# Decay scans per 128 tokens with laid-out zero columns, mirrored upper features, a first mixing in two groups, and fillers to the idlest bank

## The chip, the core and the metric

One core of a Trainium2 chip runs the whole program. The metric is device time of one execution in microseconds (us). The engines are TensorE (PE: matmuls and transposes), VectorE (DVE), ScalarE (ACT) and GpSimd (POOL); SyncE (SP) issues most of the DMAs. Each engine takes its instructions in the order of its own queue and waits on semaphores where an operand isn't ready.

## What is computed

Batch 4, 8 heads, 768 tokens, head size 48, 384 features. A linear attention with a decay per token and channel gives `x`; then comes the real part of a 2D FFT over tokens and features as mixing, a norm, and a feed-forward network (FFN) of 384 to 1536 to 384:

```python
def _attn_ref(q, k, v, alpha) -> np.ndarray:
...
    for t in range(S):
        state = alpha[:, :, t, :, None] * state + np.einsum('bhd,bhe->bhde', k[:, :, t], v[:, :, t])
        y[:, :, t] = np.einsum('bhd,bhde->bhe', q[:, :, t], state)
...
def _moe_ref(x, w_ch1, w_ch2) -> np.ndarray:
    X = np.fft.fft(x, axis=1)
    X = np.fft.fft(X, axis=2)
    mixed = np.real(X).astype(np.float32)
    u = x + mixed
    mu = np.mean(u, axis=-1, keepdims=True)
    var = np.mean((u - mu) ** 2, axis=-1, keepdims=True)
    un = (u - mu) / np.sqrt(var + 1e-06)
    ch = np.maximum(un @ w_ch1, 0.0) @ w_ch2
    return (u + ch).astype(np.float32)
```

## The kernel before, in words

**Order of the work.** Operations are not issued where they are written. A class `Plan` (from line 193) records every one with its operands and a priority, and `emit` (378) is a list scheduler: it fixes, from a table of assumed durations and delays, the order of each engine's queue and which slot each tile gets, and then issues everything from one place (L508 in the profile; relu L229). So a change of one operation can move many others. `FX` (523) names the engines that may take a kind of operation.

**Fillers.** While the planned time is below `WARM` (120 us), a planned gap of TensorE is filled with matmuls of a zero tile (L1237; one for every 0.11 us, `DUMMY`), written to a part of a PSUM bank that nothing reads. The bank is the first in a list that holds no open accumulation (466). A filler's bank may still be waiting to be read by another engine; then the filler waits, and the queue behind it.

**Attention** runs by pairs of heads (four pairs a batch; 0 to 3 are batch 0), in stages `s1` to `s8` of `attn_stages` (700). The decays of a pair are a tile `al`, 112 rows (two heads) by 768 tokens. `products` in `s1` makes running products of decays `w` by a scan on VectorE (`w<-al,d`) and the inverse weights by a second scan backwards (`al<-al,back`). The scans restart every 64 tokens: ScalarE copies every 64th decay into the scan's addend `d1` (`d<-al`), GpSimd sets these places of `al` to zero (in pair 0 VectorE does both), and since the chunks that the matmuls use have 128 tokens, VectorE multiplies the first half of each by the reciprocal of its end product (`rec`, `w<-w,rec`) and makes the decay of a chunk, `mt`, as a product of two values. `s2`, `s3` multiply keys and queries into the scans (`al<-kq,al`, `w<-kq,w`); `s4` transposes the keys (`f<-cst,al`, ScalarE copies `kt`); `s5` computes scores in a chunk and masks them (VectorE, `x<-f,cst`, in batch 0); `s6` the states, carried from chunk to chunk (`tc<-f,mt` and four steps `tc<-tc,mt`, ScalarE copies `tt`); `s7` the outputs, copied by ScalarE into the tiles `y`.

**Mixing.** The DFT over tokens is folded by sums of `y` (`combine`, 859: `z<-y,y`, `sd<-z`, `z<-sd,z`) ahead of small matmuls (`token_stage`), then the DFT over features, again by matmuls. In batch 0 `first_mix` (891) does this by groups of 128 features as soon as the pairs are there: group 0 after pair 1, group 1 after pair 2, group 2 after pair 3; each adds its part of the second stage to three open PSUM banks (`a<-f,x`, 193 and 191 columns). `adds` (976) adds the result to `y` in four VectorE steps per block of 128 rows: the lower features, and the upper ones in reversed order. The upper half of the tokens goes through a DRAM scratch (`scr`) and comes back with its rows reversed by indirect DMAs of GpSimd.

**FFN.** The weights come packed; `wsplit` (677) unpacks each block: ScalarE makes `b8` and a sign, VectorE a shift and an `or`, ScalarE an absolute value, VectorE or GpSimd a product, ScalarE the high part, VectorE or GpSimd the low part. The DMA of a further block waits until a slot is free. The norm (`norm_stages`, 1003) ends in transposes and casts to `x`; the first FFN matmul is the first `f<-x,wt`. From there the FFN of a batch and the attention and mixing of the next share TensorE.

Of the kernel before, what the change touches and what calls it, by code (L numbers as in the profile page):

```python
# [21 lines left out]
DM = H * D  # L22
# [4 lines left out]
C = 64  # L27
NW = 2 * DFF // P
NC = S // C
HM = DM // 2  # L30
CW = 112
# [22 lines left out]
SPLIT = 388  # L54
# [7 lines left out]
P4 = 512 - DM  # L62
# [40 lines left out]

def first_tables():
    p = np.arange(P, dtype=np.int64)[:, None]
    t = []
    for g in range(DM // P):
        x = 2.0 * np.pi * (((P * g + p) * np.arange(HM + 1)[None, :]) % DM) / DM
        t += [np.cos(x), np.sin(x[:, 1:HM])]
    return np.ascontiguousarray(np.concatenate(t, axis=1).astype(np.float32))  # L110
# [20 lines left out]

class View:
# [8 lines left out]
    def __getattr__(self, name):  # L141
        if name not in ("rearrange", "bitcast", "broadcast_to"):
            raise AttributeError(name)
        return lambda *a, **k: View(self.tile, self.steps + ((name, a, k),))

    def real(self, base=None):
        ap = self.tile.real if base is None else base
        for name, a, k in self.steps:
            ap = getattr(ap, name)(*a, **k)
        return ap  # L150
# [32 lines left out]
KEEP = {'c8': 0, 'a': 1, 'f1': 1, 'f2': 1, 'b8': 0, 'y': 3, 'mv': 99, 'st': 99, 'sd': 99, 'r3': 99, 'kq': 2}  # L183
# [9 lines left out]
class Plan:  # L193


    def __init__(self, engines):
        self.engines, self.ops, self.tags, self.direct, self.key, self.chain, self.fill = engines, [], {}, None, 0.0, None, False
        self.idle, self.open, self.both, self.half = None, set(), None, None
# [34 lines left out]
    def add(self, engines, name, args, kwargs):  # L233
# [8 lines left out]
        op.free, op.fill = 1, self.fill  # L242
# [135 lines left out]
    def emit(self):  # L378
# [35 lines left out]
        while placed < len(ops):  # L414
            placed += 1
            best = None
            for e, cand in wait.items():
# [17 lines left out]
                for key, n, late in sorted((ops[n].key, n, late) for t, late, n in times):  # L435
# [3 lines left out]
                    limit = min(limit, late + DELAY[e])  # L439
# [25 lines left out]
            if op.engine == "PE" and self.idle and t < self.idle[2]:  # L465
                bank = next((x for x in self.idle[3] if x not in self.open), None)
# [16 lines left out]
            for slot in op.slots:  # L483
                slot.touched.append(end)
                if slot.tag and len(slot.touched) == slot.uses:
# [37 lines left out]
FX = {'comb': 'V', 'mul': 'V', 'first': 'V', 'wm': 'VG', 'wd': 'VG', 'fold': 'V', 'ev': 'A', 'relu': 'A', 'un': 'V', 'hi': 'A', 'xh': 'A', 'er': 'AV', 'kl': 'V'}  # L523
# [4 lines left out]
def gla_mix_ffn(ctx: ExitStack, tc: tile.TileContext, alpha, kq, v, w1, w2, consts, tables, rowtab, out):  # L528
# [12 lines left out]
        "w3": ([P, 776], F32, NW3), "kt": ([P, NT - 1, CW], F32, 1),  # L541
        "z": ([P, 6, DM], F32, 1), "f": ([P, 6, DM], F32, 1), "sd": ([P, 8 * D], F32, 1), "h": ([P, S], F32R, 3), "x": ([P, 776], F32R, 6),
        "y": ([P, 3, DM], F32, NY), "b8": ([P, S], I8, 1), "c8": ([P, S], I8, 1), "st": ([P, 3, 6], F32, 2), "mv": ([P, 3, 2], F32, 2),
        "r3": ([P, 3], F32, 6),
        "al": ([P, 776], F32, NAL), "kq": ([P, 2, S], F32, NQK), "vn": ([P, VW], F32, NVN), "a": ([P, 512], F32, 3), "f1": ([P, 512], F32, 2), "f2": ([P, 512], F32, 3),
# [42 lines left out]
    mts = [fixed([P, NT], f"mt{i}") for i in range(3)]  # L588
    d1 = fixed([P, S], "d1")
    back = fixed([P, S], "back")  # L590
    rec = fixed([P, NC], "rec")
    bad = fixed([P, B * NP2], "bad")
    cm63 = fixed([P, 1], "cm63")
    ceps = fixed([P, 1], "ceps")
    zero = fixed([P, 32], "zero")
# [4 lines left out]
    scratch = [plan.fixed(dp.tile([DM, DM], F32, name=f"scr{b}")) for b in range(B)]  # L600

    def load_first():
        t, kt, vn = plan.tile("al"), plan.tile("kq"), plan.tile("vn")
        loaded.update({("al", 0): t, ("kq", 0): kt, ("vn", 0): vn})
        for lo, o in ((0, 0), (DM, SPLIT)):
            SY.dma_start(t[:, o : o + DM], alpha[0, :, lo : lo + DM])
# [5 lines left out]
    def check_first():  # L612
        t = plan.tile("h").bitcast(F32)
        SY.dma_start(t[:, 0:S], alpha[0])
        check(0, t)

    def check(p, t):
        top = t[0:CW, 0:S].bitcast(U8)[:, 3::4]
        A.activation(plan.tile("c8")[0:CW].bitcast(U8), top, AF.Square, bias=cm63[0:CW], accum_out=bad[0:CW, p : p + 1])

    def load_alpha(p):
        if p < B * NP2:
            t = plan.tile("al")
            loaded["al", p] = t
            SY.dma_start(t[:, 0:S], alpha[p])
# [18 lines left out]
    def setup():  # L644
        V.memset(zero, 0.0)
        A.activation(bs, zero[:, 0:1], AF.Sqrt)
        V.memset(d1, 0.0)
        for x in tts:
            G.memset(x, 0.0)
        V.memset(back, 0.0)  # L650
        V.memset(back[:, C - 1 :: 2 * C], 1.0)
        V.memset(cm63, -63.0)
        V.memset(ceps, 1e-6)
        for x in mts:
            V.memset(x, 0.0)
# [44 lines left out]
    def attn_stages(b, hp, i, mixed):  # L700
        tt, mt = tts[0], mts[hp % 3]
        pair = b * NP2 + hp
        e = {}
        halves = "p (c h t) -> p c h t"

        def products(lo, hi):
            as_, Af, o = loaded["al", pair], e["A"], off(lo)
            d, d2, chunks = d1[0:CW, lo:hi], back[0:CW, lo:hi], slice(lo // C, hi // C)
            if pair:
                A.copy(d[:, 0::C], as_[0:CW, o : o + hi - lo : C])  # L710
            else:
                same(d[:, 0::C], as_[0:CW, o : o + hi - lo : C])
            (G if pair else V).memset(as_[0:CW, o : o + hi - lo + 1 : C], 0.0)
            part = Af[0:CW, lo:hi]
            V.tensor_tensor_scan(out=part, data0=as_[0:CW, o : o + hi - lo], data1=d, initial=0.0, op0=ALU.mult, op1=ALU.add)
            r = rec[0:CW, chunks][:, 0::2]
            V.reciprocal(d2[:, 2 * C - 1 :: 2 * C], part[:, 2 * C - 1 :: 2 * C])
            V.reciprocal(r, part[:, C - 1 :: 2 * C])
            j0, j1 = max(lo // P - 1, 0), hi // P - 1
            V.tensor_mul(mt[0:CW, j0:j1], Af[0:CW, j0 * P + P - 1 : j1 * P : P], Af[0:CW, j0 * P + P + C - 1 : j1 * P + C : P])  # L720
            V.tensor_tensor_scan(
                out=as_[0:CW, o + hi - lo : o : -1], data0=as_[0:CW, o + hi - lo : o : -1], data1=d2[:, ::-1],
                initial=0.0, op0=ALU.mult, op1=ALU.add,
            )
            first = part.rearrange(halves, h=2, t=C)[:, :, 0]
            FL["first"].tensor_mul(first, first, r[:, :, None].broadcast_to([CW, (hi - lo) // P, C]))

        def off(t):
            return t + SPLIT - DM if pair == 0 and t >= DM else t

        def R(rows, lo, hi):
            return loaded["al", pair][rows, off(lo) + 1 : off(lo) + 1 + hi - lo]

        def times(which, x, lo, hi):
            FL["mul"].tensor_mul(x, loaded["kq", pair][0:CW, which, lo:hi], x)

        parts = ((0, DM), (DM, S)) if pair == 0 else ((0, S),)

        def s1():
            e["A"] = w3()[:, 0:S]  # L740
            if pair:
                check(pair, loaded["al", pair])
                products(0, S)
            else:
                products(0, DM)
                times(0, R(slice(0, CW), 0, DM), 0, DM)
                products(DM, S)

        def s2():
            lo = 0 if pair else DM  # L750
            times(0, R(slice(0, CW), lo, S), lo, S)

        def s3():
            for lo, hi in parts:
                times(1, e["A"][0:CW, lo:hi], lo, hi)

        def s4():
            kt = plan.tile("kt")
            e["kt"] = kt
            for a0, a1 in ((0, 3), (3, NT - 1)):  # L760
                pk = psa()
                for a in range(a0, a1):
                    T.transpose(pk[:, (a - a0) * P : (a - a0) * P + CW], R(slice(0, CW), a * P, (a + 1) * P), ident[0:CW, 0:CW])
# [3 lines left out]
        def s5():  # L767
            e["X"] = []
            for h2 in range(2):
# [4 lines left out]
                for c in range(3):  # L774
                    cs = slice((3 * h2 + c) * P, (3 * h2 + c + 1) * P)
# [612 lines left out]
```

## Time and profile before

| | us |
|---|---|
| median of 3 runs (lowest, highest) | 526.02 (525.55, 526.42) |
| the profiled execution | 527.16 |
| its span | 525.1 |
| TensorE busy (share of the span) | 503.6 (96%) |
| VectorE busy | 336.4 (64%) |
| ScalarE busy | 194.5 (37%) |
| GpSimd busy | 60.3 (11%) |

The profile is one execution. "Busy" counts instructions at work; in brackets behind a row of the timeline stands how long the engine was idle just before it and what ended that. TensorE's share is a mean over two very different parts: the head, up to the first FFN matmul, where its busy time holds the fillers, and all that follows. "PEclk" is the clock granted to TensorE, 1.00 or 0.50 in stretches of about 3.4 us.

### The profile page before, as it was taken

Reading aid. Unit: us, or ns where it says so; the run is one execution under the profiler, and the core shown is the slowest. Engines: PE = TensorE matmul, PEld = TensorE weight load, DVE = VectorE, ACT = ScalarE, POOL = GpSimd, SP = SyncE. Lnnn points to the kernel's source line nnn. Section 1 sums busy time; section 2 is a strip of 40 time slices with the busy share of each in tenths; the row PEclk is TensorE's granted clock in tenths of the full one; section 3 lists DMA queues with packets and bytes.
Section 4 is the critical chain, followed back from the end, with each engine's and each line's share of the span. In section 5 each row is a group of like instructions: output and inputs, shape, how many; then the busy total and the mean of one; then the engine's idle time right before and its main releaser. Section 6 shows DMA issues by size and latency. Waiting matters only on the chain.

```text
span 525.1 us, 10047 instructions
## 1 busy us (share of the span) xinstructions
PE 503.6 (96%) x4128; PEld 482.0 (92%) x4128; DVE 336.4 (64%) x757; ACT 194.5 (37%) x409; POOL 60.3 (11%) x84
## 2 busy tenths in 40 slices
PE   8799996999999999899999999999999999999995
PEld 7688886999999999799999999999999999999994
DVE  8878789799795798956529985755355824122112
ACT  2264566436556323634333152333322332111110
POOL 0001142042011200301212000212120000000000
PEclk9699899899999999999999999999999999999999
DMA  8992055022342510213226100120012001001001
GB/s 313 410 404 71 1 155 178 1 91 76 123 183 85 165 56 0 96 43 115 86 92 212 61 2 0 46 85 25 1 66 71 1 1 45 1 0 46 1 0 51
DMA packets 17267, 45.40 MB, mean 86 GB/s; under 512 B 1920, under 2 KB 7168, under 8 KB 17216
## 3 DMA queue, kind: packets, MB, share of 16 engines
q1 hardware_dynamic: 16160, 42.21, 22.4%
q0 software_dynamic: 768, 2.36, 1.6%
q8 instruction: 34, 0.56, 0.4%
q10 hardware_dynamic: 288, 0.13, 0.1%
q14 instruction: 17, 0.14, 0.1%
HBM read 37.62 MB, written 7.08 MB: 85 GB/s over the span
## 4 chain that ended last, share of the span: by engine, by line
PE 84%; DVE 6%; DMA 4%; ACT 3%; issue 1%; POOL 1%; SPq 0%; ACTq 0%; DVEq 0%
PE f L508 62%; PE a L508 20%; DMA wt<-in_w_dram 3%; PE f L1237 2%; DMA al<-in_alpha_dram 2%; DVE w L508 1%; DVE wt L508 1%; DVE x L508 1%; DVE y L508 1%; ACT c L508 1%; DVE tc L508 1%; ACT wt L508 0%; ACT b L508 0%; ACT f L508 0%; POOL wt L508 0%
## 5 line engine op out<-in xcount | busy, mean ns | idle before, releaser
L508 PE MATMUL f<-x,wt 128*128 128x384 f32 x864 | 180.4, 345 | 1.7 <-ACT x L508 1.7
L508 PE MATMUL f<-wt,h 128*128 128x384 f32 x864 | 176.4, 342 | 0.7 <-ACT h L229 0.7
L508 PEld LDWEIGHTS f<-x,wt 128*128 128x128 f32 x864 | 150.5, 189 | 3.7 <-ACT x L508 2.0
L508 PEld LDWEIGHTS f<-wt,h 128*128 128x128 f32 x864 | 150.3, 188 | 1.8 <-ACT h L229 1.0
L508 DVE SCALAR_TENSOR_TENSOR h<-f,h 128x384 fp32r<-128x384 f32 x96 | 53.2, 554 | 118.8 <-ACT h L229 117.9
L229 ACT ACTIVATE h<-f 128x384 fp32r<-128x384 f32 x96 | 47.2, 491 | 167.0 <-PE f L508 166.3
L508 POOL TENSOR_SCALAR_AFFINE_SELECT w<-w 128x384 f32<-128x384 f32 x48 | 34.4, 738 | 161.8 <-ACT w L508 161.8
L508 PE MATMUL a<-vn,w 128*128 128x80 f32 x288 | 43.4, 271 | 0.1
L508 PEld LDWEIGHTS a<-vn,w 128*128 128x128 f32 x288 | 39.8, 191 | 1.1 <-POOL al L508 0.2
L508 ACT COPY w<-a 128x384 f32<-128x384 f32 (+4 forms) x60 | 26.6, 481 | 33.0 <-PE a L508 31.4
L1237 PEld LDWEIGHTS f<-zero 128*32 128x32 f32 x650 | 25.9, 124 | 12.8 <-ACT x L508 3.7
L1237 PE MATMUL f<-zero 128*32 128x32 f32 x650 | 28.7, 208 | 9.1 <-ACT x L508 3.3
L508 DVE TENSOR_TENSOR_SCAN w<-al,d 112x768 f32<-112x768 f32 (+1 forms) x17 | 29.1, 1711 | 7.0 <-PE a L508 3.9
L508 DVE TENSOR_TENSOR y<-y,a 128x191 f32<-128x191 f32 (+4 forms) x106 | 30.4, 340 | 1.8 <-PE a L508 1.7
L508 DVE TENSOR_TENSOR_SCAN al<-al,back 112x768 f32<-112x768 f32 (+1 forms) x17 | 28.2, 1659 | 0.0
L508 DVE TENSOR_TENSOR z<-y,y 128x576 f32<-128x576 f32 (+1 forms) x18 | 11.8, 686 | 20.8 <-ACT y L508 20.8
L508 PE MATMUL a<-w,al 64*128 64x128 f32 (+1 forms) x288 | 22.5, 289 | 0.0
L508 PEld LDWEIGHTS a<-w,al 64*128 64x128 f32 (+1 forms) x288 | 18.0, 187 | 4.5 <-ACT w L508 2.2
L508 POOL DMA_INDIRECT y<-scr,rows x12 | 16.0, 1334 | 50.5 <-DMA scr<-y 38.3
L508 PE MATMUL a<-tt,w 112*128 112x96 f32 x120 | 21.4, 276 | 0.0
L508 DVE SCALAR_TENSOR_TENSOR tc<-tc,mt 112x48 f32<-112x48 f32 x64 | 18.7, 292 | 0.7
L508 ACT COPY y<-a 128x288 f32<-128x288 f32 x24 | 9.5, 397 | 25.6 <-PE a L508 25.6
(112 smaller groups left out, 564.4 us busy)
## 6 DMA issues: line engine op xcount, KB each, us to landing
kq<-in_kq_dram SPq DMA_DIRECT2D x13, 768.0 KB, 5.2
wt<-in_w_dram SPq DMA_DIRECT2D x8, 768.0 KB, 8.2
al<-in_alpha_dram SPq DMA_DIRECT2D x15, 384.0 KB, 5.3
out_dram<-y SPq DMA_DIRECT2D x24, 192.0 KB, 1.9
vn<-in_v_dram SPq DMA_DIRECT2D x14, 304.0 KB, 3.2
wt<-in_w_dram SPq DMA_DIRECT2D x8, 384.0 KB, 6.7
scr<-y SPq DMA_DIRECT2D x4, 576.0 KB, 3.7
wt<-in_kq_dram SPq DMA_DIRECT2D x2, 768.0 KB, 10.9
```

The source lines that it names most:

```text
L229: return lambda out, x: e.activation(out, x, AF.Relu)
L508: op.ins = op.fns[op.engine](*[real(a) for a in op.args], **{k: real(x) for k, x in op.kwargs.items()})
L1237: lambda tag, i: nc.tensor.matmul(warm[tag][i][0:32, 480:512], zero.real(), zero.real(), start=True, stop=True), 1.0, WARM,
```

## The change

1. **Scans per 128 tokens.** The host lays the decays out with a zero column ahead of each 128 tokens (tile width 776 in place of 768, a row of 129 per chunk), and the addend `d1` is a constant with a one at these columns. A scan so restarts by itself every 128 tokens, over 773 columns. `d`, the memsets of `al`, `rec`, `mt` as a product and `w<-w,rec` are gone; ScalarE copies the last column of each chunk into a new tile `over`, which serves as `mt`, and a check of `over` for overflow is added at the end.
2. **Mirrored upper features.** The host reverses the upper 192 features (weights, values, and the result), and the `y` tiles get a padding column (385 wide, set to zero by GpSimd). A reversed step over the upper half becomes a forward one, and both halves go in one instruction (`twice`). Where the second stage's banks hold sum and difference already (batch 0), `adds` is one step per block of rows; elsewhere three. Stores write two runs of 192 features per row.
3. **First mixing in two groups**, after pairs 1 and 3, each of 96 lower and the 96 mirrored upper features. `combine` works on 192 columns; new folds (`h<-z`, sum and difference of a feature and its mirror) come ahead of the token matmuls, which need 24 instructions in place of 36, with 97 rows. The second stage has 12 matmuls of 386 columns in place of 18 of 191 or 193, and two short ones per group as before.
4. **Fillers** move 48 columns in place of 32 and go to the bank whose last planned read is earliest. Some keys and delays of the planner change (`TIGHT`, `KN0`, `KEEP`).

The core of the diff:

```diff
-C = 64
...
+CP = P + 1
+AW = NT * CP + 2
+YW = DM + 1
...
+FW = 48
...
+        def products(c0, c1):
+            al, Af = loaded["al", pair][0:CW], e["A"][0:CW]
+            lo, hi = c0 * CP + 1, c1 * CP + 1
+            V.tensor_tensor_scan(out=Af[:, lo : hi - 1], data0=al[:, lo : hi - 1], data1=d1[0:CW, lo : hi - 1], initial=1.0, op0=ALU.mult, op1=ALU.add)
+            last = Af[:, lo + P - 1 : hi - 1 : CP]
+            V.reciprocal(back[0:CW, lo + P : hi : CP], last)
+            FL["mt"].copy(mt[0:CW, c0:c1], last)
+            V.tensor_tensor_scan(
+                out=al[:, hi - 1 : lo : -1], data0=al[:, hi - 1 : lo : -1], data1=back[0:CW, hi - 1 : lo : -1], initial=0.0, op0=ALU.mult, op1=ALU.add,
+            )
...
-                A.copy(d[:, 0::C], as_[0:CW, o : o + hi - lo : C])
...
-            (G if pair else V).memset(as_[0:CW, o : o + hi - lo + 1 : C], 0.0)
...
-            V.reciprocal(r, part[:, C - 1 :: 2 * C])
...
-            V.tensor_mul(mt[0:CW, j0:j1], Af[0:CW, j0 * P + P - 1 : j1 * P : P], Af[0:CW, j0 * P + P + C - 1 : j1 * P + C : P])
...
-            FL["first"].tensor_mul(first, first, r[:, :, None].broadcast_to([CW, (hi - lo) // P, C]))
...
         def s8():
             if b == 0:
                 key = plan.key
-                if hp:
+                if hp % 2:
                     plan.key += KFM
-                    first_mix(hp - 1, *mixed())
+                    first_mix(hp // 2, *mixed())
...
     def first_mix(g, ytiles, zt):
...
-        combine(ytiles, zt, g * P, P, FL["comb"])
-        zs = [zt[:, i, cols] for i in range(6)]
+        combine(ytiles, zt, g, FL["comb"])
+        c0, n = 2 * D * g, 2 * D
+        folds = []
+        for f in (V.tensor_add, V.tensor_sub):
+            x = plan.tile("h").bitcast(F32)[:, 0 : 6 * HR].rearrange("p (a n) -> p a n", a=6)
+            f(x[:, :, 1:n], zt[:, :, c0 + 1 : c0 + n], zt[:, :, c0 + HM : c0 + HM + n - 1])
+            same(x[:, :, 0 : n + 1 : n], zt[:, :, c0 : c0 + HM + n : HM + n - 1])
+            folds.append(x)
...
-            T.matmul(pm[:, HM + 1 : DM], rt[1][:, ks], t[:, HM + 1 : DM], start=g == 0, stop=False)
+            T.matmul(pm[:, 0:PQ], rt[1][0:HR, ks], sn, start=g == 0, stop=False)
...
-            V.tensor_add(lo, lo, m1)
-            first(lo[:, 1:HM], lo[:, 1:HM], m2)
-            V.tensor_add(hi, hi, m1[:, 1:HM])
-            second(hi, hi, m2)
+            both = feats(u)
+            if pms:
+                x = pm[:, HM + 1 : HM + 2].twice(-HM, HM) if flip else pm[:, 0:1].twice(HM + 2, HM)
+                V.tensor_add(both, both, x)
+                return
...
-                bank = next((x for x in self.idle[3] if x not in self.open), None)
+                bank = min((x for x in self.idle[3] if x not in self.open), key=lambda x: self.read.get(x, 0.0), default=None)
```

Two places of the queues follow. A row is one instruction or several alike (x24): output, inputs, shape, and the engines or DMA queues that it waits for; the numbers tell tiles apart.

TensorE's queue early in the head, around the output matmuls of pair 0 (`f_..<-vn,x`; `x` are masked scores), before: rows with `zero` are fillers, and bank `f_1_50` also holds the states that VectorE's first `tc` step reads.

```order
L508 MATMUL f_1_50_115<-vn_42_107,kt_6_71 48x48
L1237 MATMUL f_2_51_116<-zero 32x32 [waits DVE_49]
L1237 MATMUL f_2_51_116<-zero 32x32 x4
L508 MATMUL f_2_68_352<-vn_42_107,x_13_78 128x80 [waits PE_49]
L1237 MATMUL f_1_50_115<-zero 32x32 [waits DVE_49]
L1237 MATMUL f_1_50_115<-zero 32x32 x24
L508 MATMUL f_2_68_352<-vn_42_107,x_13_78 128x80 x3
L508 MATMUL f_0_70_392<-vn_42_107,x_14_79 128x80
```

The same place now:

```order
L1281 MATMUL f_1_48_113<-zero 32x48 x3
L530 MATMUL f_0_68_321<-vn_42_107,x_13_78 128x80 [waits DVE_49]
L530 MATMUL f_0_68_321<-vn_42_107,x_13_78 128x80 x2
L1281 MATMUL f_1_50_115<-zero 32x48 x14
L530 MATMUL f_1_69_347<-vn_42_107,x_14_79 128x80 [waits DVE_49,PE_49]
L1281 MATMUL f_1_48_113<-zero 32x48 x2
```

The fillers that waited for VectorE, one on the mask's bank and 25 on the bank of the states, are gone from ahead of the output matmuls; those in their place carry no wait, while the output matmuls themselves wait for the masks.

VectorE's queue from the scan of pair 2 (`w_2`) to the scan of pair 3 (`w_3`), before; `al_38` and `al_39` are the decays of these pairs, and a wait for Pool is one for GpSimd's memset (further `tc` steps, alike, are left out):

```order
L508 SCALAR_TENSOR_TENSOR w_2_3_68<-al_38_103,d_135 112x768 [waits DMAHW4_49,Pool_49]
L508 SCALAR_TENSOR_TENSOR tc<-tc,mt_132 112x48 [waits DVE_49]
L508 RECIPROCAL back<-w_2_3_68 112x6 [waits DVE_49]
L508 RECIPROCAL rec<-w_2_3_68 112x6
L508 TENSOR_TENSOR mt_134<-w_2_3_68 112x5
L508 SCALAR_TENSOR_TENSOR al_38_103<-al_38_103,back 112x768 [waits DVE_49]
L508 TENSOR_TENSOR w_2_3_68<-w_2_3_68,rec 112x6x64 [waits DVE_49]
L508 SCALAR_TENSOR_TENSOR tc<-tc,mt_132 112x48
L508 TENSOR_TENSOR w_1_2_67<-kq_41_106,w_1_2_67 112x768
L508 SCALAR_TENSOR_TENSOR w_3_4_69<-al_39_104,d_135 112x768 [waits DMAHW0_49,Pool_49]
```

And now, left out in the same way:

```order
L530 SCALAR_TENSOR_TENSOR w_2_3_68<-al_38_103,d_133 112x773 [waits DMAHW4_49]
L530 SCALAR_TENSOR_TENSOR tc<-tc,over 112x48 [waits DVE_49]
L530 RECIPROCAL back<-w_2_3_68 112x6 [waits DVE_49]
L530 SCALAR_TENSOR_TENSOR al_38_103<-al_38_103,back 112x773 [waits DVE_49,Activation_49]
L530 TENSOR_TENSOR w_1_2_67<-kq_41_106,w_1_2_67 112x6x128
L530 SCALAR_TENSOR_TENSOR w_3_4_69<-al_39_104,d_133 112x773 [waits DMAHW0_49]
```

The rows `rec`, `mt` and `w<-w,rec` are gone from between the two scans, and the scan of pair 3 waits for its DMA alone, no longer for GpSimd.

More of the change, by code (lines that the diff above doesn't have):

```diff
@@ L197, in __init__ @@
         self.engines, self.ops, self.tags, self.direct, self.key, self.chain, self.fill = engines, [], {}, None, 0.0, None, False
-        self.idle, self.open, self.both, self.half = None, set(), None, None
+        self.idle, self.open, self.both, self.half, self.tight = None, set(), None, None, False
+        self.read = {}
     def tag(self, name, count, make):
@@ L484, in emit @@
                 slot.touched.append(end)
+                if slot.tag in ("f1", "f2"):
+                    self.read[slot.tag, slot.cell] = end
                 if slot.tag and len(slot.touched) == slot.uses:
@@ L587, in gla_mix_ffn @@
     tc_ = fixed([P, NT - 1, D], "tc")
[L588 to L592, printed above, removed]
+    over = fixed([P, B * NP2 * NT], "over")
+    d1 = fixed([P, AW], "d1")
+    back = fixed([P, AW], "back")
+    bad = fixed([P, B * NP2 * (NT + 1)], "bad")
     cm63 = fixed([P, 1], "cm63")
     ceps = fixed([P, 1], "ceps")
-    zero = fixed([P, 32], "zero")
+    zero = fixed([P, FW], "zero")
     ones = fixed([P, 1], "ones")
@@ new lines, in R, with Aq, times, s1 @@
+        def R(rows, c):
+            return loaded["al", pair][rows, c * CP + 2 : c * CP + 2 + P]
+        def Aq(rows, c):
+            return e["A"][rows, c * CP + 1 : c * CP + 1 + P]
+        def times(which, x, o, c0, c1):
+            y = span(x[0:CW], c0, c1, o)
+            k = loaded["kq", pair][0:CW, which, c0 * P : c1 * P].rearrange("p (c t) -> p c t", t=P)
+            FL["mul"].tensor_mul(y, k, y)
+        parts = ((0, 3), (3, NT)) if pair == 0 else ((0, NT),)
+        def s1():
+            e["A"] = w3()
@@ L726, in products @@
-            FL["first"].tensor_mul(first, first, r[:, :, None].broadcast_to([CW, (hi - lo) // P, C]))
[L728 to L747, printed above, removed]
+                check(pair, span(loaded["al", pair], 0, NT, 0))
@@ L897, in first_mix @@
         for part in range(2):
[L898 to L900 removed]
+            pr = psa()[0:HR]
+            kn = token_stage(pr, [folds[part][:, i] for i in range(6)], part)
+            FL["er"].copy(rt[part][0:HR, 0:kn], pr[:, 0:kn])
         if g == 0:
             first["pm"] = [plan.tile("a") for _ in range(3)]
[L903 to L904 removed]
+        t = first["t"][0:HR, g * FT_W : (g + 1) * FT_W]
+        co, sn = t[:, 0 : HM + 1], t[:, HM + 1 : FT_W]
+        last = g == 1
         for m in range(3):
@@ L1101, in store_for, with two @@
     def store_for(dst):
-        return lambda blk, m, u: SY.dma_start(dst[blk, m], u)
+        return lambda blk, m, u: SY.dma_start(dst[blk, m].rearrange("p (s n) -> p s n", s=2), u)
     sequence = {}
+    def two():
+        ys = [plan.tile("y") for _ in range(2)]
+        G.memset(ys[1][:, :, HM : HM + 1], 0.0)
+        return ys
     def batch(b):
@@ L1108, in mixed @@
             if b not in sequence:
[L1109 removed]
+                sequence[b] = (two(), plan.tile("z"))
             return sequence[b]
```

224 lines of the change are left out of this document (121 added, 103 removed).

## The prediction, made before the changed kernel had run

> **What bounds the kernel now.** First the windows view (stretch, its length, busy us and count of TensorE's matmuls, its weight loads, VectorE, ScalarE and GpSimd, then the granted clock, the DMA share and GB/s), cut at the start of the first FFN matmul (92.81 us) and at the end of the last matmul (518.65; the span ends at 525.10):
>
> ```profile
> 0.00:92.81 92.81, 80.80 (x1098) 72.19 (x1098) 76.49 (x192) 47.25 (x88) 14.29 (x17) 0.93 0.59 217
> 3.35:75.21 71.86, 65.14 (x806) 58.09 (x805) 58.57 (x130) 33.84 (x66) 9.00 (x9) 0.91 0.61 230
> 92.81:518.65 425.84, 422.77 (x3034) 409.78 (x3031) 259.35 (x564) 147.24 (x322) 45.99 (x67) 1.00 0.17 58
> ```
>
> From 92.81 on TensorE is busy 422.77 of 425.84 us and nothing else is near it. The change leaves the matmuls of that stretch as they are, so it stays 425.84 + 6.45 = 432.29 us unless something newly starves TensorE. Everything is decided by F, the start of the first FFN matmul. In the 92.81 us before it TensorE's 80.80 are partly fillers (zero matmuls); the same view for their line alone:
>
> ```profile
> 0.00:92.81 92.81, 27.68 (x636) 25.07 (x636) 0.93 0.59 217
> 17.00:30.00 13.00, 7.56 (x149) 6.91 (x149) 0.61 1.03 404
> ```
>
> One filler is two records: 27.68 / 318 = 87 ns each, and 101 ns in 17 to 30 us. Without them the head holds 53.1 us of work and 12.0 us idle, so TensorE waits there for others. Second view, the chain of waits up to F (start us, us, what):
>
> ```profile
> 74.25 0.97 DVE wt L508
> ...
> 75.27 4.91 DMA wt<-in_w_dram
> ...
> 82.86 1.84 POOL wt L508
> 84.72 4.56 DMA wt<-in_w_dram
> 89.36 0.88 ACT b L508
> 90.24 1.02 ACT c L508 x2
> 91.26 0.75 ACT x L508 x2
> ```
>
> VectorE ends unpacking the fourth weight block at 75.21; that frees the slot for a weight DMA, which feeds ScalarE and GpSimd, which free the slot of the next. From 75.21 to F are 17.6 us. Before 75.21 VectorE is the queue that must run dry. Third view, its waits from the first load to there (us in total, times, longest):
>
> ```profile
> DVE x L508 <- PE f L508: 4.7, 3, 2.5
> DVE w L508 <- POOL al L508: 2.6, 1, 2.6
> DVE wt L508 <- ACT wt L508: 2.2, 2, 1.7
> DVE x L508 <- PE f L1237: 2.2, 1, 2.2
> DVE z L508 <- ACT y L508: 1.4, 1, 1.4
> ```
>
> That is 13.1 us of waits beside 58.57 busy. So F = start + VectorE's work + its waits + 17.6.
>
> **The change, part by part.** *VectorE's work up to that row.* Two rows of its timeline (start us, us, instruction), then groups by form (count, busy us, mean ns of one):
>
> ```profile
> 3.70 0.96 DVE L508 TENSOR_TENSOR_SCAN w<-al,d 112x384 f32<-112x384 f32 x1
> 4.57 0.20 DVE L508 TENSOR_SCALAR cst<-cst 128x128 int32<-128x128 int32 x1
> ...
> L508 DVE TENSOR_TENSOR w<-w,rec 112x384 f32<-112x384 f32 x15 | 8.3, 555 | 0.0
> L508 DVE TENSOR_TENSOR z<-z,sd 128x192 f32<-128x192 f32 x12 | 3.9, 347 | 0.0
> L508 DVE TENSOR_TENSOR z<-f 128x570 f32<-128x570 f32 x6 | 4.2, 745 | 0.0
> L508 DVE TENSOR_TENSOR z<-y,y 128x384 f32<-128x384 f32 x6 | 3.1, 551 | 1.4 <-ACT y L508 1.4
> L508 DVE TENSOR_TENSOR z<-z,sd 128x128 f32<-128x128 f32 x6 | 1.5, 282 | 0.0
> ```
>
> An instruction starts about 0.08 us before its forerunner ends (3.70 + 0.96 against 4.57), so each costs its duration less 0.08. Gone for four pairs: the multiplies by `rec` (three of 384 at 0.47, two of 192 at 0.25: -1.9) and the small `rec`, `mt`, `d` and memset rows (about -1.0). Sums of `y`: six of 384 columns at 0.47 and 24 of 128 at 0.20 become four of 576 at 0.67 (as 570 columns) and 16 of 192 at 0.27: 7.6 to 7.0. Added: the folds into `h`, two of 570 at 0.67 and two small ones: +1.5; and one more weight step stands ahead of the row (+0.9). Scans grow from 768 to 773 columns: nothing. Together -1.1. I write 57.4. The first scan can start at 3.4 instead of 3.70, so without any wait the row would end at 60.8.
>
> *The 2.6 us wait for `al`, and what made it*, from the timelines of the four engines (in brackets the idle time ahead, and what ended it):
>
> ```profile
> 16.87 2.27 PE L1237 MATMUL f<-zero 128*32 128x32 f32 x50 [3.04 <-DVE tc L508]
> ...
> 23.90 0.69 ACT L508 COPY kt<-f 128x336 f32<-128x336 f32 x2 [6.98 <-PE f L508]
> ...
> 25.67 0.12 POOL L508 MEMSET al<- 112x13 f32 x1 [8.57 <-ACT d L508]
> ...
> 25.82 1.76 DVE L508 TENSOR_TENSOR_SCAN w<-al,d 112x768 f32<-112x768 f32 x1 [2.57 <-POOL al L508]
> ```
>
> A filler wrote to a bank that VectorE had yet to read; TensorE stood 3.04 us behind it, the `kt` transposes came late, ScalarE's `kt` copies too, and behind them in ScalarE's queue stood the copy `d`, then GpSimd's memset, then the scan of pair 3. The changed kernel has neither copy nor memset, and these fillers wait for nothing. ScalarE's new copy `over` is read only by `tc` steps that come later. The wait goes whole; next late is the load of that pair's decays, issued at 9.46; the second row is the group's median time to landing:
>
> ```profile
> 9.46 0.33 SPq L508 DMA_DIRECT2D al<-in_alpha_dram  x1
> ...
> al<-in_alpha_dram SPq DMA_DIRECT2D x5, 384.0 KB, 9.8
> ```
>
> 9.46 + 9.8 = 19.3 is earlier than VectorE gets there (about 21), so it costs nothing.
>
> *The other 10.5 us.* 4.7 are mask steps waiting for score matmuls, 2.2 a copy behind a filler, the rest ScalarE's copies. All come from TensorE and ScalarE running behind VectorE, and both were set back by the stall above. In the new order VectorE has weight or sum rows ahead of most of them. Bounds: none is left (F = 60.8 + 17.6 = 78.4) or all are (88.9). I keep the wait for `y` (1.4, its ScalarE copies stay) and the shortest mask wait (0.8): 2.2, nearer to the first end, since their common source is gone. F = 60.8 + 2.2 + 17.6 = 80.6.
>
> *TensorE's own sum must not exceed that.* Four runs of its timeline, the last of them from the steady part:
>
> ```profile
> 65.89 3.06 PE L508 MATMUL a<-f,x 128*128 128x191 f32 x16
> 68.78 4.57 PE L508 MATMUL f<-cst,z 128*128 128x65 f32 x40
> ...
> 81.22 5.38 PE L1237 MATMUL f<-zero 128*32 128x32 f32 x164
> ...
> 129.22 0.78 PE L508 MATMUL a<-vn,kt 128*64 128x48 f32 x20
> ```
>
> Token matmuls go from 36 to 24: 12 x 4.57 / 20 = -2.7. The second stage goes from 18 matmuls of about 192 columns (three groups of 3.06 us with two short ones each, so some 0.43 each) to 12 of 386 (0.86): +2.1. Fillers: 308 before F, with 48 columns instead of 32. At full clock a filler of 32 takes 66 ns (5.38 / 82) and a real matmul of 48 columns 78 ns (0.78 / 10, its last drain included), so I leave the mean at 87: 26.8. The sum is 53.1 - 0.6 + 26.8 = 79.3, plus 3.3 of idle that no filler waited in: 82.6 at the clock of before. But the clock may differ (windows as above, TensorE alone):
>
> ```profile
> 14.37:17.78 3.41, 0.91 (x29) 1.00 0.99 401
> 17.78:21.19 3.41, 3.41 (x37) 0.50 1.03 412
> ...
> 24.60:28.02 3.42, 3.42 (x63) 0.50 1.03 400
> 55.33:58.74 3.41, 2.49 (x27) 1.00 0.02 5
> 58.74:62.16 3.42, 3.42 (x19) 0.50 0.00 0
> 92.88:96.29 3.41, 3.27 (x21) 0.50 0.03 5
> ```
>
> The window with the 3 us stall was followed by three at half clock, 17.78 to 28.02; a window with 2.49 of 3.41 us busy was followed by one too. The 13.65 us at half clock ahead of F hold 6.8 us of lost speed, so TensorE's sum lies between 75.8 and 82.6, and 80.6 is inside. The Trainium skill ("TensorE: Matmul & The Clock Gate", Why this matters for your kernels) asks for no idle gap over about 3 us, and by that rule the head would now run at full speed throughout, rival 2 below. The trace agrees for 17.78, not for 58.74, ahead of which TensorE idled 0.92 us in all; nor does it agree with that page's table of two states (Part 1), which has one busy window restore the clock, since here it took three.
>
> *Behind 75.21* the chain has the same members. ScalarE's check copy `c` now stands ahead of the last unpacking instead of behind it. Both are in the chain either way, but `c` reads decays that SP issues behind that weight block; if they land later, the unpacking, the `x` casts and F wait for the difference: 0 to 1 us (the 1.02 of `c` itself). I take 0. The `y` adds in this part shrink from 24 to 6 wide ones (six of 384 columns at 0.47 for 24 of about 192 at 0.27, -3.7); they ran beside the chain, so I count nothing, and lose nothing if the longer second stage (+2.6 us in the last group) uses that up.
>
> *Elsewhere:* fewer VectorE rows and 15 fewer GpSimd memsets of 0.12 us after F lie beside a busy TensorE: nothing. Stores become two runs per row, of 768 B; the tail of 6.45 us holds the last: between 0 and +0.3, I take 0.
>
> **The sum.** Span 80.6 + 432.3 = 512.9; the profiled execution took 527.16 for a span of 525.10, so 515.0; the median of the runs shown (526.02) is 1.14 lower, which gives 513.8 us, 12.2 below.
>
> **The rivals.**
> 1. *The waits stay.* They belong to the round trips between VectorE, TensorE and ScalarE, not to the stall. F = 88.9, time 522.1. For it: 4.7 us are waits for real matmuls, and 13 us of 72 is much. Against: 10.5 us follow one stall.
> 2. *The clock is full in the head.* F = 78.4 and 1.7 us less for the half-clock window that followed F in the old trace (92.88): 509.9. For: the stall is gone. Against: the window at 55.33.
>
> 3. *Slower: fillers become TensorE's bound.* If their time goes with the columns, 87 ns becomes 131, 308 of them 40.3, and TensorE's sum 53.1 - 0.6 + 40.3 + 3.3 = 96.1: every filler stands in order ahead of a matmul of the chain. Time 96.1 + 433.2 = 529.3. It loses to before from 120 ns a filler on. For: the 101 ns at half clock. Against: the 78 ns of the real 48-column matmuls.
> 4. *Nothing net.* F comes earlier, but the second half's weights or the next batch's attention aren't ready and TensorE idles later: 526. Against: VectorE has 259 of 426 us busy there, and does no more than before.
>
> **How the numbers follow.** A measurement of this kernel (half range 0.43 us of 526) tells about 0.2%, 1.05 us. Forecast, F from 77.5 to 84.5 (510.7 to 517.7): 0.58. Waits stay, 517.7 to 524.9: 0.17. Full clock, below 510.7: 0.12. Slower by fillers: 0.08. Nothing net: 0.05. Faster is 0.58 + 0.17 + 0.12 = 0.87, same 0.05, slower 0.08. The range 508.5 to 522.5 leaves out the 0.13 of the last two rivals, and some 0.06 in the tails of the first two.
>
> **What would show it.** Right: the first FFN matmul near 80.6; no fillers waiting for `tc`; the pair 3 scan at about 21 with no wait for GpSimd; VectorE's waits up to the fourth weight block near 2 us; 432 us behind F. Wrong: mask waits of 4 us or more (rival 1), PEclk 1.0 in all head windows (2), TensorE busy without idle up to an F beyond 90 (3), or idle TensorE after F (4).

## The result, and the profile after

The changed kernel takes 511.51 us (median of 4 runs, 510.82 to 513.03) against 526.22 for the kernel before beside it: a ratio of 0.9722 (0.9693 to 0.9751). The forecast was 513.8. A ratio leaves out executions over 1.5% slower than the fastest of their kernel, while medians and ranges hold all. The profiled execution has a span of 510.2 us, 14.9 less than before.

The page's lines of TensorE and of the granted clock, before (a digit is a slice of 13 us, the head is the first seven):

```profile
PE   8799996999999999899999999999999999999995
PEclk9699899899999999999999999999999999999999
```

The page's first lines and the same two lines of the changed kernel:

```profile
span 510.2 us, 9785 instructions
PE 500.4 (98%) x4060; PEld 476.6 (93%) x4060; DVE 326.3 (64%) x661; ACT 193.7 (38%) x407; POOL 59.5 (12%) x72
...
PE   9999999999999999999999999999999999999993
...
PEclk9999999999999999999999999999999999999997
```

Before, TensorE's slices of the head went from six to nine tenths and the clock had three dips, the third just behind the head; now both are at nine tenths or more up to the last slice. The windows view of the changed kernel has the same stretches as in the prediction, cut at its own events (the head, VectorE's stretch, from the first FFN matmul to the last, the tail):

```profile
0.00:80.80 80.80, 79.25 (x1038) 68.24 (x1038) 73.83 (x150) 45.49 (x84) 10.39 (x12) 1.00 0.68 249
3.49:63.77 60.28, 60.11 (x788) 52.59 (x786) 56.35 (x106) 32.74 (x63) 1.82 (x1) 1.00 0.72 271
80.80:502.49 421.69, 421.13 (x3023) 408.34 (x3023) 251.97 (x512) 148.26 (x324) 49.13 (x60) 1.00 0.18 59
502.49:510.20 7.71, 0.00 (x1) 0.00 (x0) 0.53 (x2) 0.00 (x0) 0.00 (x0) 0.64 0.28 86
```

So F, the first FFN matmul, starts at 80.80 (before 92.81): -12.0. From F to the last matmul 421.69 us pass in place of 425.84: -4.15, since TensorE's idle time there went from 3.07 to 0.56 us and the half-clock window right behind F (3.27 us busy, 1.6 of them lost) is gone. The tail is 7.71 in place of 6.45: +1.26. The sum is -14.9, the difference of the spans.

VectorE's waits up to its fourth weight block, and the scan of pair 3, in the changed kernel:

```profile
DVE x L530 <- PE f L530: 2.8, 6, 0.6
DVE w L530 <- DMA al<-in_alpha_dram: 1.0, 2, 0.7
DVE z L530 <- ACT y L530: 0.5, 1, 0.5
```

```profile
21.85 1.77 DVE L530 TENSOR_TENSOR_SCAN w<-al,d 112x773 f32<-112x773 f32 x1
...
62.89 0.95 DVE L530 TENSOR_TENSOR wt<-wt,wt 128x768 fp32r<-128x768 f32 x1
```

The 13.1 us of waits are 4.3, of which 0.7 are the first load. The scan of pair 3 starts at 21.85 (before 25.82) and waits for nothing. The fourth weight block ends at 63.8 (forecast 63.0, before 75.21).

But the chain of waits no longer runs through the weight DMAs. Its last pieces ahead of F:

```profile
58.72 3.03 PE a L530 x10
61.75 3.77 PE f L1281 x86
65.53 2.64 PE f L530 x24
68.16 1.39 PE f L1281 x30
69.56 5.01 PE a L530 x16
...
77.38 1.21 ACT f L530 x2
...
80.80 0.45 PE f L530
```

It is TensorE itself, fillers included (L1281 is their line now), then the norm. The fillers' own busy time in the head says the same:

```profile
0.00:80.80 80.80, 32.75 (x616) 29.78 (x616) 1.00 0.68 249
```

308 fillers took 32.75 us, 106 ns each, more than the 27.68 us before, and TensorE idles only 1.55 us ahead of F. So the changed kernel's head has another limit than the prediction's sum, and F came out near 80.6 all the same. The experiments are to tell which part of the change is worth what, and why the two wrong terms met.

### The profile page after: what moved, and what is told of

Read it like the earlier page. It is cut to its first block, busy times and chain, and to the rows that moved or that the text cites. A ratio compares the mean times of both kernels' runs of the same rounds, so it can differ in the third digit from the quotient of the medians.

```text
span 510.2 us, 9785 instructions
## 1 busy us (share of the span) xinstructions
PE 500.4 (98%) x4060; PEld 476.6 (93%) x4060; DVE 326.3 (64%) x661; ACT 193.7 (38%) x407; POOL 59.5 (12%) x72
## 4 chain that ended last, share of the span: by engine, by line
PE 92%; DMA 3%; DVE 1%; ACT 1%; issue 0%; SPq 0%; ACTq 0%; DVEq 0%
PE f L530 64%; PE a L530 22%; PE f L1281 5%; DMA kq<-in_kq_dram 1%; DMA wt<-in_w_dram 1%; DMA al<-in_alpha_dram 1%; DVE y L530 1%; ACT c L530 0%; ACT f L530 0%; ACT b L530 0%; DVE al L530 0%; DVE w L530 0%; ACT y L530 0%; DVE r L530 0%; ACT tt L530 0%
## 5 line engine op out<-in xcount | busy, mean ns | idle before, releaser
L1281 PE MATMUL f<-zero 128*32 128x48 f32 x622 | 33.2, 215 | 1.1 <-DVE zero L530 1.1
L1281 PEld LDWEIGHTS f<-zero 128*32 128x32 f32 x622 | 30.1, 116 | 4.3 <-issue 1.5
L530 DVE TENSOR_TENSOR_SCAN w<-al,d 112x773 f32<-112x773 f32 (+1 forms) x17 | 28.6, 1685 | 1.0 <-DMA al<-in_alpha_dram 1.0
L530 DVE TENSOR_TENSOR_SCAN al<-al,back 112x773 f32<-112x773 f32 (+1 forms) x17 | 29.0, 1705 | 0.1
L530 DVE TENSOR_TENSOR y<-y,a 128x191 f32<-128x191 f32 (+3 forms) x65 | 25.5, 428 | 1.9 <-PE a L530 1.5
L530 DVE TENSOR_TENSOR y<-y,f 128x384 f32<-128x384 f32 x30 | 15.6, 553 | 8.5 <-PE f L530 8.5
L530 DVE TENSOR_TENSOR z<-y,y 128x576 f32<-128x576 f32 x16 | 11.5, 754 | 14.5 <-ACT y L530 14.5
L530 DVE SCALAR_TENSOR_TENSOR tc<-tc,over 112x48 f32<-112x48 f32 x64 | 20.1, 314 | 0.6
## 6 DMA issues: line engine op xcount, KB each, us to landing
wt<-in_kq_dram SPq DMA_DIRECT2D x2, 768.0 KB, 11.3
```

Of the source, the lines that this page charges most:

```text
L530: op.ins = op.fns[op.engine](*[real(a) for a in op.args], **{k: real(x) for k, x in op.kwargs.items()})
L1281: lambda tag, i: nc.tensor.matmul(warm[tag][i][0:32, 512 - FW : 512], zero.real()[:, 0:32], zero.real(), start=True, stop=True), 1.0, WARM,
```

## The experiments

The edits to the fillers leave every other instruction in its place on its engine, so these runs differ in the fillers alone. Two runs carry the scans over to the kernel before, alone and with the filler edits. The runs were made in three groups, each with the kernel before beside it: 527.0 us in the first group (the first four runs below), 524.8 in the second (the next four), 526.7 in the third.

**Both filler edits on the kernel before.** In `Plan` and the filler's matmul of the kernel before:

```diff
-                bank = next((x for x in self.idle[3] if x not in self.open), None)
+                bank = min((x for x in self.idle[3] if x not in self.open), key=lambda x: self.read.get(x, 0.0), default=None)
...
-    zero = fixed([P, 32], "zero")
+    zero = fixed([P, 48], "zero")
```

> The kernel before with both filler edits alone (48 columns, and the bank whose last planned read is earliest); every other instruction and its order stay as in before. Theory A (the stall behind one filler, and what it set back, made most of VectorE's waits): the 3.0 us stall at 13.8 to 16.9 us goes, F (start of the first FFN matmul) comes 5 to 9 us earlier than 92.8, ratio 0.983 to 0.990. Rival B (the scans without copy, memset and the multiplies by rec, and the mixing in two groups, made the gain): F moves by at most 2 us, ratio 0.996 to 1.003. Rival C (wider fillers cost as much as they save): slower, ratio above 1.003.

Measured: 527.34 us (520.38 to 528.76 in 10 runs), ratio 1.0021 (0.9976 to 1.0066). The profiled execution was the fastest of them (520.38): F at 88.2, full clock in every slice, 4.5 us of waits for the masks left. The other nine reach up to 528.8, and the granted clock on record for each parts them: the four at 520.4 to 525.2 have a mean of 0.992 to 0.997, the six at 527.3 to 528.8 one of 0.981 or 0.982. So the clock still dipped in six of ten. Rival B's ratio came true, though the profiled execution showed theory A's F. The fillers alone are worth nothing in the median.

This profile also tests the prediction's reason for the waits: the stall is gone and the clock full, and VectorE's waits up to its fourth weight block (71.3 us) still hold 4.5 us for masks, 2.4 for ScalarE's weight rows and 1.5 for `y`, 8.4 of the 10.5 us before.

**Both filler edits undone in the changed kernel.**

```diff
-FW = 48
+FW = 32
...
-                bank = min((x for x in self.idle[3] if x not in self.open), key=lambda x: self.read.get(x, 0.0), default=None)
+                bank = next((x for x in self.idle[3] if x not in self.open), None)
```

> The changed kernel with both filler edits undone (32 columns, first free bank of the list); all other instructions in the order of the changed kernel. Theory A: the stall is back at the same place, half-clock windows follow, F 86 to 89 instead of 80.8, time 517 to 520. Rival B: F within 2 us of 80.8, time 510 to 513.5. Rival D (the wider fillers are now the limit, and narrower ones free TensorE): F below 79, time under 510.

Measured: 517.85 us (516.01 to 519.36), ratio 0.9864 (0.9793 to 0.9934), F at 81.33. The time fits theory A, the F does not: it is rival B's. TensorE's timeline in this run shows the stall, shorter, and a second one ahead of F:

```profile
15.34 1.07 PE L1281 MATMUL f<-zero 128*32 128x32 f32 x28 [1.83 <-DVE tc L530]
...
80.13 1.27 PE L1281 MATMUL f<-zero 128*32 128x32 f32 x20 [2.27 <-ACT x L530]
```

The stall by the `tc` bank cost little here. What the old fillers cost stands behind F: 4.6 us more from F to the last matmul than in the changed kernel, with the clock halved from about 79 to 86 us. A window with 1.41 of 3.40 us busy came just ahead:

```profile
75.70:79.10 3.40, 1.41 (x16) 1.00 0.33 130
79.10:82.50 3.40, 2.27 (x27) 0.52 0.00 0
82.50:85.90 3.40, 3.40 (x13) 0.50 0.00 0
```

**No fillers in the changed kernel.**

```diff
-WARM = 120.0
+WARM = 0.0
```

> The changed kernel without any filler; all other instructions in the same order. Theory A (waits between the engines set F, the fillers only fill): F 77 to 82, time 508 to 513, even with half-clock windows, since TensorE has about 47 us of real work in the head. Rival E (the clock sets F): half clock in most head windows, F 84 or later, time 515 or more, and a slow start of the FFN. Rival D (fillers overrun their gaps): F below 77, time under 508.

Measured: 528.73 us (519.16 to 533.28). F is at 93.9 in the profile, VectorE waits 16.1 us for masks, and the clock is on record as halved at 78 to 81 and 91 to 98 us. It was halved for much longer. The trace's first record of the clock, a change to full, stands at 64.03 us here (at 3.8 to 6.9 us in every run with fillers); ahead of it the views print full clock because nothing is on record. The same 14 token matmuls, ahead of that record here and at full clock in the changed kernel:

```profile
60.74 2.94 PE L530 MATMUL f<-cst,h 128*97 128x65 f32 x14
```

```profile
48.79 1.60 PE L530 MATMUL f<-cst,h 128*97 128x65 f32 x14
```

In the last run below, where half clock is on record, the same 14 also take 2.94 us. Within this run, four of `f<-wt,x` took 1.03 us at 55.07 and 0.60 us at 69.08. So TensorE ran at half clock up to 64 us. Rival E came true in the mechanism and in the time, and in the median the whole gain of the change is gone. Theory A is wrong in that the fillers only fill.

**Fewer fillers in the changed kernel.**

```diff
-DUMMY = 0.11
+DUMMY = 0.15
```

> The changed kernel with one filler per 0.15 us of planned gap instead of 0.11 (221 fillers, not 311); all other instructions in the same order. In the changed kernel 308 fillers took 32.75 us, 106 ns each, and TensorE idled 1.6 us in the head: if their overrun sets F (rival D), F falls by 2 to 4 us, time 507.5 to 509.5, as long as PEclk stays 1.0. If VectorE's work sets F (theory A), F stays within 0.7 us of 80.8, time 510.8 to 512.2. If the thinner filling lets the clock fall (rival E), time over 513.

Measured: 508.97 us (507.97 to 511.71), ratio 0.9695 (0.9641 to 0.9748), F at 76.90 in the profile, no half clock ahead of it (one window behind it, at 119.9 us). Rival D came true: F moved from 80.80 to 76.90 when nothing but 89 fillers, 88 of them ahead of F, were taken out. VectorE's waits for masks fell to 0.6 us.

**The scans alone on the kernel before**: the laid-out decays, the constant `d1`, `over` and its check, without `rec`, `d`, the memsets and `w<-w,rec`; the mixing and the fillers are those of before. The core:

```diff
+            V.tensor_tensor_scan(out=Af[:, lo : hi - 1], data0=al[:, lo : hi - 1], data1=d1[0:CW, lo : hi - 1], initial=1.0, op0=ALU.mult, op1=ALU.add)
...
-            (G if pair else V).memset(as_[0:CW, o : o + hi - lo + 1 : C], 0.0)
...
-            FL["first"].tensor_mul(first, first, r[:, :, None].broadcast_to([CW, (hi - lo) // P, C]))
```

> The kernel before with the scans per 128 tokens alone (laid-out decays, no copy d, no memset of al, no rec and w<-w,rec, the check of over); mixing in three groups, features not mirrored, fillers as before. After the two runs that split off the fillers, F is 81.3 with all parts but the fillers changed and 92.8 before. Theory F (the scans made that): F 81 to 84 in the profile, time 516 to 520. Rival G (the mixing in two groups and the shorter adds made it): F 88 or later, time 522 or more.

Measured: 528.32 us (526.55 to 531.80), ratio 1.0071 (1.0024 to 1.0117): a little slower than before. Rival G's bounds hold (F 94.3), but not because the scans won nothing. VectorE's timeline of this run shows that they did what the prediction said of them, and what ate it:

```profile
21.27 1.76 DVE L508 TENSOR_TENSOR_SCAN w<-al,d 112x773 f32<-112x773 f32 x1
...
36.14 2.14 DVE L508 TENSOR_TENSOR x<-f,cst 128x384 int32<-128x384 int32 x4 [0.83 <-PE f L508]
...
56.04 0.56 DVE L508 TENSOR_TENSOR x<-f,cst 128x384 int32<-128x384 int32 x1 [2.84 <-PE f L508]
64.78 0.96 DVE L508 TENSOR_TENSOR wt<-wt 128x768 f32<-128x768 f32 x1 [3.45 <-ACT wt L508]
```

The scan of pair 3 starts 4.55 us and the masks of pair 2 4.1 us earlier than before (25.82, 40.21). Then, in the first group's mixing, TensorE waits 1.69 us for VectorE's copy `x` of the token stage. VectorE is late because one small sum, 0.28 us long elsewhere, takes 1.92 us while GpSimd runs a weight step:

```profile
48.17 1.92 DVE L508 TENSOR_TENSOR sd<-z 128x128 f32<-128x128 f32 x1
48.01 1.92 POOL L508 TENSOR_TENSOR wt<-wt 128x768 f32<-128x768 f32 x1 [9.68 <-ACT wt L508]
51.69 1.03 PE L1230 MATMUL f<-zero 128*32 128x32 f32 x16 [1.69 <-DVE x L508]
```

Each of the four profiles with three groups has one such row in the head, 1.82 to 1.92 us long, which ends 0.06 to 0.16 us behind a GpSimd weight step; no profile with two groups has one ahead of F. That GpSimd's step stretches it is read from this overlap; no run moved that step. TensorE's windows behind it read:

```profile
48.20:51.60 3.40, 1.79 (x17) 1.00 0.00 0
51.70:55.10 3.40, 3.34 (x25) 0.51 0.00 0
55.10:58.50 3.40, 3.40 (x17) 0.50 0.00 0
...
65.40:68.80 3.40, 3.40 (x13) 0.50 0.26 94
```

Half clock from 51.8 to 68.8 us, with TensorE full. These 17 us of work would take an estimated 8.5 at full clock: more than the 4.5 us that were won. Two shorter stretches at half clock stand at 17.6 to 21.0 and, around F, at 92.7 to 99.5 us.

**One filler edit each in the changed kernel**, narrow fillers with the new bank, and wide ones with the old bank.

```diff
-FW = 48
+FW = 32
```

> The changed kernel with fillers of 32 columns, still to the bank read earliest. Theory H (the width keeps the clock up, the bank removes the waits): no filler waits but half-clock windows in the head or right behind F, time 513 to 517. Rival I (the bank alone is what helps; narrow fillers only cost less): F 77 to 79, PEclk 1.0 in the head, time 507 to 510.

Measured: 510.48 us (509.96 to 510.91), ratio 0.9722 (0.9691 to 0.9753), F at 77.70, full clock. Rival I is right on F and the clock; the time is half a microsecond above what it gave.

```diff
-                bank = min((x for x in self.idle[3] if x not in self.open), key=lambda x: self.read.get(x, 0.0), default=None)
+                bank = next((x for x in self.idle[3] if x not in self.open), None)
```

> The changed kernel with fillers of 48 columns to the first free bank of the list. Theory H: fillers wait for VectorE and ScalarE by some 5 us in all as in the run with both filler edits undone, clock mostly full, time 512 to 516. If the bank matters little: 510.5 to 512.

Measured: 516.30 us (514.61 to 517.30), ratio 0.9830 (0.9794 to 0.9867), F at 84.33, full clock, fillers waiting 5.9 us in all, 1.1 of them at the start. Theory H's time ended at 516; the bank is worth 4.6 us against the changed kernel beside it, which follows. With the new bank the width is worth nothing that these runs show: narrow fillers have the earlier F, and their ratio can't be told from the changed kernel's.

**The changed kernel again**, beside the three runs above.

> The changed kernel itself once more, beside the others on one chip, for its spread and a second profile: 510 to 513.5, F 79.5 to 82.

Measured: 511.66 us (510.72 to 511.97), ratio 0.9742 (0.9711 to 0.9774), F at 79.96. The same run of 43 fillers ahead of the second group's token matmuls shows the width's price at full clock, in the changed kernel and in the one with narrow fillers:

```profile
61.68 3.84 PE L1281 MATMUL f<-zero 128*32 128x48 f32 x86
```

```profile
58.95 2.91 PE L1281 MATMUL f<-zero 128*32 128x32 f32 x86
```

That is 89 and 68 ns a filler, 22 ns for 16 columns.

**The scans and both filler edits on the kernel before**, so the changed kernel less the mirrored features, the mixing in two groups and the planner's changed keys (`TIGHT`, `KN0`, `KEEP`).

> The kernel before with the scans per 128 tokens and both filler edits; mixing still in three groups, features not mirrored. The scans alone gave F 94.3 with half clock from 51.5 to 69, the filler edits alone F 88.2 at full clock in the profiled run. Theory J (parts multiply: at full clock the scans are worth what they moved the scan of pair 3, 4.5 us): F 83 to 85.5, time 514.5 to 518, and the mixing in two groups is worth the rest, 3 to 4 us. Rival G (only the mixing counts): F 87 or later, time 520 or more. Rival K (the mixing counts for nothing): F 80 to 82, time 510 to 513.

Measured: 519.97 us (513.12 to 521.54 in 4 runs), ratio 0.9810 (0.9740 to 0.9881). In the profile F is at 89.5, and the dip is there again at nearly the same place, behind a window with 2.50 of 3.40 us busy, whose idle time is a wait of 0.90 us for the same copy:

```profile
49.90:53.30 3.40, 2.50 (x25) 1.00 0.00 0
53.40:56.80 3.40, 3.40 (x18) 0.52 0.00 0
...
63.60:67.00 3.40, 3.40 (x12) 0.50 0.78 263
```

By its median rival G holds (F 87 or later, 520). The one execution of 513.12 is near rival K. It was not profiled, but its mean granted clock is on record: 0.998, against 0.983 to 0.985 in the other three. So it ran without the dip, which is worth about 7 us here.

**Other densities of fillers in the changed kernel**: 0.15 us again, 0.19 us, and 0.13 us with 32 columns.

```diff
-DUMMY = 0.11
+DUMMY = 0.19
```

> The changed kernel with one filler per 0.15 us once more, beside other densities on one chip: 508 to 510, F 76 to 78.

> The changed kernel with one filler of 48 columns per 0.19 us of planned gap. Fillers no longer overrun their gaps at 0.15, so nothing more is won in the queue: if the clock holds, 508 to 510; if thinner filling lets it fall (theory E), 512 or more with half-clock windows.

> The changed kernel with fillers of 32 columns, one per 0.13 us of planned gap. F 76 to 78 as in the run with 48 columns per 0.15; if width is what holds the clock, some runs are 4 us or more above the lowest, if it is busy time alone, 507.5 to 510.

Measured: 0.15 gives 508.43 (507.27 to 509.62), ratio 0.9653 (0.9623 to 0.9683); 0.19 gives 510.29 (507.63 to 516.24), 0.9703 (0.9649 to 0.9756); 32 columns at 0.13 give 514.58 (509.95 to 535.27), 0.9738 (0.9694 to 0.9781). The medians are between 508 and 515, but the spread grows as the fillers thin out: 2.4, 8.6 and 25 us. The clock on record goes with it: at 0.19 the three executions below 509 us have a mean of 0.992 to 0.995, the three from 512.0 to 516.2 one of 0.976 to 0.986; with 32 columns at 0.13 it is 0.992 to 0.994 up to 511.8 us and 0.978 or 0.981 at 514.6 and 515.2. So both outcomes that were named for 0.19 occur, and with 32 columns some executions are 4 us and more above the lowest, as was named for the case that the width holds the clock. That isn't settled by it, since 258 fillers of 32 columns and 171 of 48 move nearly the same number of columns ahead of F. The last run's profile is of its 531.28 us execution and shows such a dip:

```profile
20.20:23.60 3.40, 2.23 (x27) 1.00 1.04 383
23.70:27.10 3.40, 3.40 (x28) 0.50 1.04 413
```

From there the clock stayed halved until 71.5 us. With fewer fillers of 48 columns (0.15) F was at 77.1 and the head held 24.18 us of them:

```profile
0.00:77.10 77.10, 24.18 (x440) 21.48 (x440) 1.00 0.71 261
```

At 0.19 F is at 77.12, so from 0.15 on the fillers no longer set it. What does, by the chain of the run with 0.15, is VectorE's sums, folds and weight rows (56 to 64 us), then the second stage (to 70 us), then the load of the next decays, for which ScalarE's check copy `c` waits 0.23 us.

The version with 0.15 beats both kernels here: its interval, 0.9623 to 0.9683, lies below that of the changed kernel in the second group of runs, 0.9711 to 0.9774. The two did not run side by side, and the interval of 0.15 in the first group, 0.9641 to 0.9748, overlaps.

The medians together, in us (the last row holds the planner's changed keys as well, which no run parts from the mirror and the two groups):

| | old fillers | new bank alone | 48 columns alone | both |
|---|---|---|---|---|
| kernel before | 524.8 to 527.0 | | | 527.3 |
| with the scans | 528.3 | | | 520.0 |
| with scans, mirror and two groups | 517.9 | 510.5 | 516.3 | 511.5 and 511.7 |

## Why the prediction was right, and where it was right by luck

The range held, and F came out at 80.80 against 80.6. Point by point:

- **VectorE's work** without waits to the fourth weight block: forecast to end at 60.8. It ended at 63.8 with 3.6 us of waits behind the first load, so 60.2 without them. Right.
- **The wait for `al` goes whole.** Right: the scan of pair 3 starts at 21.85 (forecast about 21), at 21.27 with the scans alone. That the load would not be late was right too.
- **The other 10.5 us of waits shrink to 2.2, "since their common source is gone".** The size was near (3.6), the reason was wrong. The source was said to be the stall behind one filler. With the stall still there (1.83 us, both filler edits undone) F was 81.3; with the stall gone and nothing else changed, 8.4 of the 10.5 us stayed and the median did not move. What the waits do follow is TensorE's speed: with two groups the mask waits up to 60 us are 0.6 to 3.1 us where TensorE had full clock and fillers, 11.3 and 13.1 us in the two profiles at half clock there. And the kernels with three groups lose the clock in the middle of the head: at 58.7 us before, 51.8 with the scans, 53.5 with scans and both filler edits; the exception is the 520 us execution with both filler edits. With two groups only the profile with thin narrow fillers (from 23.7 us) and the one without fillers (up to 64 us) are at half clock there. The VectorE row beside GpSimd's weight step is what all three-group profiles share; with the scans it makes all the idle time of the window ahead of the dip, before only 0.29 of its 0.92 us. So it is part of the cause at most, and no run isolates it.
- **TensorE's sum.** "I leave the mean at 87" for a filler failed: it is 106. The 87 ns already hold a head partly at half clock; at full clock fillers of 32 columns have a mean of 84 ns (25.95 us for 308, narrow fillers with the new bank), and 16 columns more cost 22. Fillers took 32.75 us, not 26.8. The real work was 79.25 - 32.75 = 46.5 us; the forecast was 52.5 at the clock of before, or 45.7 at full clock. So two errors of 6 us cancelled: fillers dearer, clock full. The sum "at the clock of before" was 82.6, at full clock 75.8, and the measured 79.25 + 1.55 lies between because of these two, less 1.7 us of idle time.
- **What sets F.** Forecast: VectorE's chain of weights. Measured: TensorE's queue with the fillers in it. Taking out 88 fillers ahead of F moved it by 3 to 4 us (80.80 and 79.96 with them), though no other instruction changed its place. Without them, F is 76.9 to 77.1, below the 78.4 that the prediction gave for no wait at all. So that F met 80.6 is luck, though VectorE's rows are next in line, at 77. The step that the prediction put at nothing, `c` waiting for its decays, cost nothing in the changed kernel.
- **Rival 1**, the waits stay: no. **Rival 2**, full clock in the head: its condition came true (PEclk 1.00 from 6.29 us on), its time did not, since the dearer fillers took the gain; with the sparser fillers its 509.9 is about what comes out (508.4 and 509.0). **Rival 3**, fillers become TensorE's bound: its mechanism is the one at work, at 106 ns and not at the 131 that it feared, so below its own turning point of 120. **Rival 4**: no; behind F the time fell by 4.15 us.
- **The clock rule.** The Trainium skill ("TensorE: Matmul & The Clock Gate", Why this matters for your kernels) asks for no idle gap over about 3 us. Without fillers the median rose by 17 us, and gaps of 3.26 and 3.58 us were followed by half clock (at 77.7 and 91.3 us), so its aim is borne out, but its bound is not: windows with 1.8 to 2.5 of 3.4 us busy were followed by half clock in four kernels (before, scans, scans with both filler edits, 32 columns at 0.13), and the longest single gaps in them were 0.6 to 1.7 us. The prediction's reading that the clock took three windows to return holds for the dip at 17.78 alone; after the one at 58.74 it took one.
- **The tail.** Forecast 0 to +0.3, taken as 0; it is +1.26. All mirrored kernels have 7.5 to 8.0 us there, the others 6.45 to 6.7. SyncE's issue of the last three stores, before and after:

```profile
518.11 1.37 SPq L508 DMA_DIRECT2D out_dram<-y  x3
```

```profile
501.95 1.88 SPq L530 DMA_DIRECT2D out_dram<-y  x3
```

 Half a microsecond of the tail is the longer issue of two runs per row; the rest wasn't taken apart. The stores' packets in that stretch went from 432 to 816 for the same bytes.
- **Behind F.** Forecast unchanged, measured -4.15 us: the half-clock window (1.6, which rival 2 had counted) and 2.5 us of idle time.

What stays open: what exactly sets the granted clock. In the kernel before, a window with 1.75 of 3.41 us busy (86.05 to 89.46) was followed by full clock, one with 2.49 by half. And which of the mirror, the two groups and the planner's keys is worth the 8 us between 520.0 and 511.5 us: no run takes them one by one, and the two groups without the scans were not tried.

## What to carry to other kernels

Changes of a kernel's head were not additive here, where TensorE's clock fell behind thin windows: the scans alone made it 0.7% slower, the fillers alone nothing, all together 2.8% faster. So look at the granted clock of each variant before blaming or praising an edit, and take several executions with the mean clock of each, since they show a dip that one profile misses; and where a trace's first record of the clock comes late, time the same matmul on both sides of it. A filler is work in an in-order queue: price it at the clock that it keeps, fill a gap with less than fits, and write it to a bank that nobody still has to read.

## What the runs showed of the hardware that was not expected

- Return to full clock took one window of 3.4 us in some places (58.74 to 62.16 and 92.88 to 96.29 in the kernel before) and far longer in others, though TensorE was busy nearly throughout: three windows in the kernel before (17.78 to 28.02), four with scans and both filler edits (53.5 to 67.2), fourteen in the last run (23.7 to 71.5). Without fillers, with a few gaps of up to 2.1 us, it came at 64 us. The Trainium skill ("TensorE: Matmul & The Clock Gate", Part 1) has one busy window restore it; the trace agrees in the first two places and not in the others.
- Every profiled execution starts at half clock, though the views print 1.00 there. Fillers of 48 columns start every 160 ns up to the trace's first record of the clock (6.29 us in the changed kernel) and every 85 ns behind it; those of 32 columns every 107 and 64 ns, and 160 and 107 ns are also what they take where half clock is on record. So the first run of 63 fillers took 7.99 us, 127 ns each, where later ones take 89.
